# Fillers on a matrix of ones from the start, two of the first four attention jobs in layer 1's buffers, and x's halves squared apart

## The chip, the core and the metric

The kernel runs on one core of one Trainium2 chip. TensorE (PE) multiplies into eight PSUM banks; VectorE (DVE), ScalarE (ACT) and GpSimd (POOL) do the element work; SyncE (SP) issues every DMA. The metric is device time in microseconds for one launch. The time before is the median of three runs.

## What is computed

The reference is attention with decay followed by two pairs of dense layers, all in float32:

```python
# q, k, v: 4 batches x 8 heads x 576 x 64, f: 4 x 8 x 576
cum = np.cumsum(np.log(np.clip(f, 1e-4, 1)), axis=-1)
scores = q @ k.T / 8 + cum[..., :, None] - cum[..., None, :]     # causal
attn = exp(scores - max) / (sum + 1e-9)
x = (attn @ v).transpose(0, 2, 1, 3).reshape(2304, 512)
h = x @ w1_in;  x = (h * sigmoid(h)) @ w1_out        # 512 -> 2048 -> 512
h = x @ w2_in;  x = (h * cos(h)) @ w2_out            # 512 -> 2048 -> 512
```

## The kernel before

**Work and tiles.** Attention is cut into jobs of two heads. Sixteen jobs of kind "a" (four per batch) do the first 256 rows of a sequence as one unit "c01", sixteen of kind "b" the other 320 rows as three units. The tokens are cut into nine tiles of 256; tile j needs the four jobs of its batch and kind. Each of the two layers does, for each tile, eight steps: a step takes 256 columns of the hidden layer, multiplies (line 1282, "h", 24 products), applies the activation, and multiplies into the output (line 1394 in layer 1, line 1183 in layer 2, "y"). Layer 1 runs tiles 0 and 1 step by step beside each other; layer 2 follows layer 1.

**Operands.** Float32 operands that are multiplied as 16-bit ones are split: a high half rounded (name "chi") and a low half, the rest ("clo", for x "xlo", both on line 334). The scale of a split comes from a sum of squares: ScalarE squares with a running sum (line 339), VectorE adds two of those ("sc", line 406), TensorE sums them over partitions by a product with a matrix of ones (line 410, tile "nrm"), VectorE makes powers of two of it (lines 415 to 417). Weights come as 64-bit words and are put into float32 by an exponent shift ("cexp", ScalarE or GpSimd, line 314 or 316), a low-bits step ("cb1", line 462 or 465) and two VectorE steps (lines 468 and 472).

**A unit of attention** (`unit_tasks`): TensorE makes the scores into two PSUM banks "st" (line 746, after mask rows of line 740), VectorE adds the decay, writes the weights tile "e" and keeps the extreme (line 757, "max"), ScalarE takes the exponentials with their sums (line 777), VectorE the reciprocals (lines 783 and 784), then the normalisation goes to GpSimd, VectorE or ScalarE ("nm", lines 314 and 316), TensorE transposes (line 794, "tt"), ScalarE or VectorE copies ("pt"), TensorE multiplies with v (line 928, "pv"), and the product goes to x. For jobs 0 to 3 the decays do not come by DMA: TensorE spreads them ("dp", line 690) as soon as the cumulated sums are there (line 433), and ScalarE copies them ("dk").

**What sets the order.** Each step is a task with an engine (or a choice of engines), a planned duration, a key, the tasks that it waits for, and buffers that it takes (`acq`) and gives back (`rel`); how many buffers there are stands in `TOK`: four PSUM banks "s" for scores, decays, transposes, sums and output units alike, two banks "h" for layer 1, four "e", two "x" for the split x tiles. `Scheduler.run` plays the tasks through once while the program is built, against planned times, and takes for each engine the ready task with the lowest key; the order that results is the program, each engine's queue being fixed from then on. The planner has a rule for TensorE's clock: work takes twice its time until a stretch of it was busy enough. Where TensorE has nothing ready between the planned times `FILL0` and `FILL1`, it gets a filler product `turn` (line 391, tile "spin", bank y0), whose result nobody reads:

```python
    def turn():
        nc.tensor.matmul(spin, identb, one.unsqueeze(1).to_broadcast([128, 2, 256]), start=True, stop=True, ...)
```

**x.** `split_tasks` makes the two halves of an x tile: two squares, one scale, then for each 512-column half a "chi" and an "xlo". Tiles 0 and 1 are written by jobs 0 to 7 straight into SBUF ("x_165", "x_166" in the order), two jobs for each half.

Of the kernel before, what the change touches and what calls it, by code (L numbers as in the profile page):

```python
# [9 lines left out]
F32 = mybir.dt.float32  # L10
# [27 lines left out]
QD = 3  # L38
W1 = 32
CK2 = 20  # L40
FILL0 = 8.0
FILL1 = 60
GAP4, GAP8 = 8, 16
CK0, CK1 = 4, 1.4
# [17 lines left out]
LAND = {"cload": 2.0, "w2l": 1.5, "ldq": 1.5, "ldd": 2.0, "xd": 2.0, "ldx": 1.5, "xt": 1.5}  # L62
ENG = ("PE", "ACT", "DVE", "POOL", "SP")
NEG = -8.0e9
MK2 = -1500.0
EARLY, LATE = 110, ()
KDEC, KDP = 12.0, -0.5
# [10 lines left out]
class Scheduler:  # L78
# [36 lines left out]
    def run(self):  # L115
# [4 lines left out]
        busy = {e: 0.0 for e in ENG}  # L120
        dma_free, lanes, wake = 0.0, [], 0.0
        events, cnt, done = [], 0, 0
        warm, win, work, two = False, 0, [0.0], 0.0

        def push(t, kind, x):
            nonlocal cnt
# [40 lines left out]
        while events:  # L167
# [17 lines left out]
            while progress:  # L185
                progress = False
                for e in ENG:
# [37 lines left out]
                    if e == "PE":  # L225
                        w = int(now / HAM)
                        while win < w:
                            warm = work[win] > 0.7 * HAM
                            win += 1
                            if len(work) <= win:  # L230
                                work.append(0.0)
                        if not warm:
                            end += best.dur
                        a = now
                        while a < end - 1e-9:
                            w = int(a / HAM + 1e-9)
                            while len(work) <= w:
                                work.append(0.0)
                            b = min(end, (w + 1) * HAM)
                            work[w] += b - a  # L240
                            a = b
# [22 lines left out]
def c_dve(n, psum=False):  # L264
    return (0.13 if psum else 0.07) + n / 960
# [31 lines left out]
def decay_attention_silu_cos_kernel(ctx, tc, qa, qb, f, w1i, w1o, w2i, w2o, out):  # L297
# [90 lines left out]
    spin = ps.tile([128, 512], F32, tag="y0", bufs=1, name="spin")  # L388

    def turn():  # L390
        nc.tensor.matmul(spin, identb, one.unsqueeze(1).to_broadcast([128, 2, 256]), start=True, stop=True,  # L391
                         skip_group_check=True)
    sd.keep_warm(0.215, turn)

# [316 lines left out]
    def unit_tasks(jb, kind, pos, split, rel):  # L711
# [7 lines left out]
        dma = jb.kind == "b" and jb.x  # L719
        cell = {}  # L720

        def bank(name):
            return ps.tile([128, 512], F32, tag="s", bufs=TOK["s"], name=name)

        def f_s():
            cell["sm"] = sbt("su", [128, 16])
            for a in range(2):
                st[a] = bank("st")
            for a in range(heads):
                e[a] = sbt("e", [128, S], name="e")  # L730
            if tail:
                for n, (x, y) in enumerate(PASS):
                    mm(st[0][:, 0:256], jb.tail[x], jb.k[y][:, 0:256], start=n == 0, stop=n == 2, skip_group_check=True)  # L733
# [115 lines left out]

        i = pos  # L850
        pe = {"c01": 0.9 if jb.n < ND else 0.72, "c2": 0.5, "c3": 0.67, "T": 0.76}[kind]
        ts = add("PE", pe, f_s, split + [masked], key=i - 10000.0, acq=["s", "s"] + ["e"] * heads + ["su"], rel=rel, name="S")
        te, tm = [], []
        for a in range(2):
            d = {"c01": 0.78, "T": (0.45, 0.52)[a]}.get(kind, c_dve(w) + 0.15)
            hidden = [] if tail and not a else jb.masked[kind]
            t = add("DVE", d, lambda a=a: f_max(a), hidden + ([ts] if not (tail and a) else [ts, t]), key=i + 0.1 * a, rel=["s"],
                    name="max")
            tm.append(t)
            if not tail or a:  # L860
                h = 0 if tail else a
                te.append(add("ACT", (0.9 if kind == "c01" else c_act(w) + 0.19), lambda h=h: f_exp(h), [t], key=i + 0.1 * h,
                              name="exp"))
# [16 lines left out]
        for a in range(0 if dma else heads):  # L880
            tn = []
            for j, (o, n) in enumerate(((0, 128), (128, 256)) if kind == "c01" else ((0, w),)):
                k = 2 * a + j if kind == "c01" else a
                def nf(eng, a=a, o=o, n=n, k=k):
                    return lambda: f_norm(eng, a, o, n, k)
                tn.append(add("POOL", c_pool(n, True), nf("POOL"), [tr], key=i + 0.1 * a, name="nm",
                              alts=[("DVE", c_dve2(n), nf("DVE")), ("ACT", c_act(n) + 0.09, nf("ACT"))]))
            nb = 5 if tail else w // 128
            t = add("PE", 0.115 * nb, lambda a=a: f_t(a), tn + [jb.first], key=i + 0.1 * a - 15000.0,
                    acq=["s"] * (2 if tail else 1) + (["pt"] if kind in ("c01", "c3") and a == 0 else []), rel=["e"],  # L890
                    name="T")
            jb.first = jb.first or t
            for h in range(2 if tail else 1):
                b = h if tail else a
                n = (512, 128)[h] if tail else w
                r.append(add(**copies(lambda b=b: dst(b), lambda b=b: src(b), n, ("ACT", "DVE"), psum=True),
                             deps=[t], key=i + 0.1 * a, rel=["s"], name="tc"))
# [61 lines left out]
    for kind, b in ORDER:  # L959
        if kind == "a":  # L960
            pos += {1: GAP4, 2: GAP8}.get(b, 0)
        for hp in range(H // 2):
# [3 lines left out]
            jb.pt = jb.xo = jb.first = jb.qk = None  # L966
            jb.mate = mate if kind == "a" and hp % 2 else None
            mate = jb
            sp = load_tasks(jb, pos)
            if kind == "a":  # L970
                jb.un = unit_tasks(jb, "c01", pos, sp, [])
                jb.end = pv_tasks(jb, pos + 1, jb.un)
                if jb.mate:
                    add("SP", 0.0, lambda: None, jb.un + jb.mate.un, key=-300, rel=["dk", "qk"])
                    add("SP", 0.0, lambda: None, [jb.end, jb.mate.end], key=-300, rel=["v"])
                pos += 2
            else:
                un = []
                for i, u in enumerate(("c3", "c2", "T")):
# [124 lines left out]
    def split_tasks(l, j, deps, key):  # L1104
# [5 lines left out]
        def make():  # L1110
            x_t[l, j] = sbt("x", [128, 2, KD, TB], F16, "x")
        r = []
        q = [add(**squares(lambda c=c: raw(c), 512, sq[:, c, k:k + 1]), deps=deps, key=key, name="sqx") for c in range(2)]
        ts = scale_tasks(k, q, key)
        tm = add("SP", 0.0, make, [ts], key=-300, acq=["x"])
        for c in range(2):
# [353 lines left out]
```

## Time and profile before

| | us |
|---|---|
| median of 3 runs | 919.29 (917.72 to 922.87) |
| the profiled execution | 919.6 |
| its span | 917.6 |
| TensorE busy in it | 902.0 |
| first TensorE instruction | 6.59 |
| first layer-1 product | 50.89 |

The page gives the busy time of each engine over the span; the stage table gives it for stretches of it. A stretch in which TensorE is busy throughout can still hold fillers, or products at half the clock. The chain of waits follows the work that ended last back from the end; a wait is put down to what released it. Line numbers are those of the kernel before; the change shifts them by 4 to 13.

### The profile page before, as it was taken

Reading aid. Unit: us, or ns where it says so; the run is one execution under the profiler, and the core shown is the slowest. Engines: PE = TensorE matmul, PEld = TensorE weight load, DVE = VectorE, ACT = ScalarE, POOL = GpSimd, SP = SyncE. Lnnn points to the kernel's source line nnn. Section 1 sums busy time; section 2 is a strip of 40 time slices with the busy share of each in tenths; the row PEclk is TensorE's granted clock in tenths of the full one; section 3 lists DMA queues with packets and bytes.
Section 4 is the critical chain, followed back from the end, with each engine's and each line's share of the span. In section 5 each row is a group of like instructions: output and inputs, shape, how many; then the busy total and the mean of one; then the engine's idle time right before and its main releaser. Section 6 shows DMA issues by size and latency. Waiting matters only on the chain.

```text
span 917.6 us, 20983 instructions
## 1 busy us (share of the span) xinstructions
PE 902.0 (98%) x7930; PEld 754.5 (82%) x7930; DVE 768.6 (84%) x1884; ACT 694.2 (76%) x1406; POOL 145.7 (16%) x228
## 2 busy tenths in 40 slices
PE   7998999999999999999999999999999999999997
PEld 4577777777887877878888888888888888888886
DVE  6999989868877999999898966887888888788775
ACT  6999997777877988898787746776676676676663
POOL 5873222112111422232010000000000000000000
PEclk9999999999999999999999999999999999999999
DMA  9876356778996977875756787000001000000010
GB/s 346 296 259 183 90 160 178 172 158 178 205 190 168 255 222 236 201 220 155 241 202 203 261 296 250 27 24 24 25 24 48 25 24 24 1 25 24 1 25 24
DMA packets 113701, 130.03 MB, mean 142 GB/s; under 512 B 63872, under 2 KB 76160, under 8 KB 113600
## 3 DMA queue, kind: packets, MB, share of 16 engines
q1 hardware_dynamic: 113600, 128.70, 48.7%
q8 instruction: 62, 1.02, 0.5%
q14 instruction: 39, 0.32, 0.1%
HBM read 90.25 MB, written 24.72 MB: 125 GB/s over the span
## 4 chain that ended last, share of the span: by engine, by line
PE 90%; DVE 4%; ACT 3%; DMA 2%; issue 1%; POOL 0%; SPq 0%; DVEq 0%; ACTq 0%; POOLq 0%
PE h L1282 38%; PE y L1394 19%; PE y L1183 18%; PE pv L928 3%; PE spin L391 2%; PE tt L794 2%; PE st L753 2%; PE pv L917 2%; PE st L746 2%; PE dp L690 1%; PE st L734 1%; DMA v<-qb 1%; PE st L733 0%; DVE eh L818 0%; ACT junk L339 0%
## 5 line engine op out<-in xcount | busy, mean ns | idle before, releaser
L1282 PE MATMUL h<-x,wi 128*128 128x256 f16 x3456 | 407.5, 273 | 0.0
L1282 PEld LDWEIGHTS <-wi 128*128 128x128 f16 x3456 | 334.2, 98 | 46.5 <-issue 6.7
L1394 PE MATMUL y<-g,rw 128*128 128x256 f16 (+1 forms) x1600 | 224.8, 292 | 0.5 <-ACT g L314 0.5
L1183 PE MATMUL y<-wo,g 128*128 128x256 f16 x1512 | 176.4, 273 | 0.0
L1183 PEld LDWEIGHTS <-g 128*128 128x128 f16 x1512 | 147.9, 98 | 17.1
L1394 PEld LDWEIGHTS <-rw 128*128 128x128 f16 x1344 | 129.3, 98 | 18.2 <-issue 3.1
L1336 ACT ACTIVATE t<-h,ru 128x512 f32<-128x512 f32 x72 | 49.4, 685 | 68.4 <-PE h L1282 68.3
L777 ACT ACTIVATE e<-e,su 128x128 f32<-128x128 f32 (+4 forms) x144 | 82.6, 576 | 9.2 <-DVE su L757 8.0
L1361 DVE TENSOR_TENSOR g<-t,g 128x896 f16<-128x896 f32 x72 | 78.4, 1089 | 10.0 <-ACT g L1358 6.5
L1342 ACT ACTIVATE t<-t,ru 128x512 f32<-128x512 f32 x72 | 51.7, 718 | 37.2 <-DVE t L1339 37.2
L1346 DVE SCALAR_TENSOR_TENSOR t<-h,rg,t 128x512 f32<-128x512 f32 x72 | 53.9, 749 | 29.7 <-ACT t L1343 29.5
L1339 DVE SCALAR_TENSOR_TENSOR t<-t,ru,h 128x512 f32<-128x512 f32 x72 | 53.6, 745 | 24.5 <-ACT t L1336 24.4
L1358 ACT ACTIVATE g<-t 128x896 f16<-128x896 f32 x72 | 67.5, 937 | 6.5 <-DVE t L1352 6.3
L757 DVE CUSTOM_DVE_ANT_0 e<-st,dk 128x256 f32<-128x256 f32 (+3 forms) x144 | 64.3, 477 | 7.5 <-PE st L753 2.8
L1307 ACT ACTIVATE t<-h,rg 128x512 f32<-128x512 f32 x72 | 48.8, 678 | 27.5 <-PE h L1282 26.9
L314 ACT ACTIVATE g<-t,rg 128x512 f16<-128x512 f32 (+1 forms) x70 | 50.1, 716 | 23.9 <-PE y L1394 18.6
L1310 DVE SCALAR_TENSOR_TENSOR t<-t,h 128x512 f32<-128x512 f32 x72 | 49.2, 683 | 15.2 <-ACT t L1307 14.7
L1394 PEld LDWEIGHTS y<-g,rw 128*128 128x128 f32 x256 | 46.7, 194 | 11.0 <-issue 3.4
L334 DVE SCALAR_TENSOR_TENSOR g<-t,rg,g 128x512 f16<-128x512 f32 x56 | 43.2, 772 | 12.9 <-ACT g L314 12.5
L1343 ACT ACTIVATE t<-t,halfpi 128x512 f32<-128x512 f32 x72 | 52.0, 722 | 2.3
L818 DVE SCALAR_TENSOR_TENSOR eh<-e,su,eh 128x512 f16<-128x512 f32 (+2 forms) x66 | 40.5, 639 | 2.9 <-ACT eh L314 2.3
L316 POOL TENSOR_SCALAR e<-e,su 128x128 f32<-128x128 f32 (+3 forms) x38 | 24.7, 656 | 68.0 <-DVE su L784 33.9
(157 smaller groups left out, 1259.7 us busy)
## 6 DMA issues: line engine op xcount, KB each, us to landing
rw<-w1i SPq DMA_DIRECT2D x16, 512.0 KB, 4.5
rw<-w1o SPq DMA_DIRECT2D x16, 512.0 KB, 8.7
x<-x_d SPq DMA_DIRECT2D x16, 512.0 KB, 4.2
dk<-decay_d SPq DMA_DIRECT2D x16, 512.0 KB, 4.8
raw<-w2i SPq DMA_DIRECT2D x16, 512.0 KB, 5.7
raw<-w2o SPq DMA_DIRECT2D x16, 512.0 KB, 4.8
qs<-qb SPq DMA_DIRECT2D x16, 480.0 KB, 4.0
w2o_d<-w SPq DMA_DIRECT2D x24, 256.0 KB, 3.5
```

The lines of the kernel that those rows point to most:

```text
L314: nc.scalar.activation(dst, src, AF.Copy, scale=scale)
L757: nc.vector.tensor_tensor_reduce(out, s, d, -0.125, first, ALU.add, ALU.min, cell["sm"][:, o:o + 1])
L777: nc.scalar.activation(x, x, AF.Exp, bias=sm[:, i:i + 1], scale=-1.0, accum_out=sm[:, 4 + i:5 + i])
L1183: nc.tensor.matmul(y[bank][:, 256 * half:256 * half + 256], g[:, gi, ga], w[:, wi, 256 * col:256 * col + 256], start=p == 0 and half == 0 ...
L1282: nc.tensor.matmul(h[:, i], w[:, wi, 128 * k:128 * k + 128], x[:, xi, k], start=(i == 0 and q == 0 and k == 0), stop=(i == 1 and q == 2 an ...
L1339: nc.vector.scalar_tensor_tensor(cell["t"], cell["t"], r, cell["h"], ALU.subtract, ALU.subtract)
L1342: nc.scalar.activation(cell["t"], cell["t"], AF.Abs, scale=r)
L1343: nc.scalar.activation(cell["t"], cell["t"], AF.Sin, scale=-2.0 * PI, bias=halfpi)
L1346: nc.vector.scalar_tensor_tensor(cell["t"], cell["h"], r, cell["t"], ALU.mult, ALU.mult)
L1358: nc.scalar.activation(g_t[s][:, 0], cell["w"], AF.Copy)
L1361: nc.vector.tensor_tensor(g_t[s][:, 1], cell["w"], g_t[s][:, 0], ALU.subtract)
L1394: nc.tensor.matmul(y[:, e * TB:(e + 1) * TB], w[:, wi, 128 * ec:128 * ec + 128], g[:, gi, i * TB:(i + 1) * TB], start=(st and e == 0), sto ...
```

## The change

- Fillers: `FILL0` goes from 8.0 to 1.5, and the filler multiplies the matrix of ones with itself in place of the identity and the mask tile, so it needs VectorE's first memset alone (GpSimd writes the identity).
- The planner's clock rule: full speed comes after two busy stretches in a row in place of one.
- `ABREAST = (1, 3)`: jobs 1 and 3 take their scores in the two "h" banks and their weights in one of the two "x" buffers, in place of two "s" banks and two "e" tiles; the x buffer is given back once both heads' transposes are done.
- The planned duration of "max" in a c01 unit goes from 0.78 to 0.6.
- `split_tasks`: with four jobs behind a tile, the squares of half c wait for jobs 2c and 2c+1 alone.
- `HEAD = 0` is added and does nothing at that value.

```diff
-FILL0 = 8.0
+FILL0 = 1.5
+HEAD = 0
+ABREAST = (1, 3)
...
-                            warm = work[win] > 0.7 * HAM
+                            full2 = work[win] > 0.7 * HAM
+                            warm = full2 and (warm or half)
+                            half = full2
...
-        nc.tensor.matmul(spin, identb, one.unsqueeze(1).to_broadcast([128, 2, 256]), start=True, stop=True,
+        nc.tensor.matmul(spin, ones16, ones16.unsqueeze(1).to_broadcast([128, 4, 128]), start=True, stop=True,
...
+        early = kind == "c01" and jb.n in ABREAST
...
-                st[a] = bank("st")
+                st[a] = bank("st") if not early else ps.tile([128, 512], F32, tag="h", bufs=2, name="st")
+            both = sbt("x", [128, 2, KD * TB], F16, name="e").bitcast(F32) if early else None
-                e[a] = sbt("e", [128, S], name="e")
+                e[a] = both[:, a] if early else sbt("e", [128, S], name="e")
...
-        ts = add("PE", pe, f_s, split + [masked], key=i - 10000.0, acq=["s", "s"] + ["e"] * heads + ["su"], rel=rel, name="S")
+        ts = add("PE", pe, f_s, split + [masked], key=i - 10000.0, acq=["h", "h", "x", "su"] if early else ["s", "s"] + ["e"] * heads + ["su"],
+                 rel=rel, name="S")
-            d = {"c01": 0.78, "T": (0.45, 0.52)[a]}.get(kind, c_dve(w) + 0.15)
+            d = {"c01": 0.6, "T": (0.45, 0.52)[a]}.get(kind, c_dve(w) + 0.15)
...
+            if early:
+                add("SP", 0.0, lambda: None, [t, jb.first], key=-300, rel=["x"] if a else [])
...
-        q = [add(**squares(lambda c=c: raw(c), 512, sq[:, c, k:k + 1]), deps=deps, key=key, name="sqx") for c in range(2)]
+        q = [add(**squares(lambda c=c: raw(c), 512, sq[:, c, k:k + 1]), deps=deps[2 * c:2 * c + 2] if len(deps) == 4 else deps, key=key,
+                 name="sqx") for c in range(2)]
```

Three places show how the order moves. First the start of TensorE's queue; dp is the spread of the decays, st a score bank. Before:

```order
L690 MATMUL dp_202<-cum_163,sel_158 128x256 x2
L690 MATMUL dp_211<-cum_163,sel_158 128x256 x2
L740 LDWEIGHTS one_133
L740 MATMUL st_226<-one_133 128x2x128
...
L746 MATMUL st_246<-qk_168 128x256
```

After (the first two rows stand there ten times):

```order
L395 LDWEIGHTS ones16_136
L395 MATMUL spin_159<-ones16_136 128x512
L694 MATMUL dp_214<-cum_163,sel_158 128x256 x2
L694 MATMUL dp_223<-cum_163,sel_158 128x256 x2
L747 LDWEIGHTS one_133
L747 MATMUL st_236<-one_133 128x2x128
...
L753 MATMUL st_256<-qk_168 128x256
```

Ten fillers stand ahead of the first decays; up to the first layer-1 product 79 others follow, where 99 stood before.

Second, VectorE's queue behind the scores of jobs 0 and 1 (su_225 and su_244 before, su_235 and su_254 after, hold those jobs' sums; st_333, st_306 are job 2's scores, st_326 and st_327 job 3's; rw are weights in conversion). Before:

```order
L783 TENSOR_SCALAR su_225<-su_225 128x4
L784 RECIPROCAL su_225<-su_225 128x4
L406 SCALAR_TENSOR_TENSOR sq16_140<-sq_139 128x1
L468 SCALAR_TENSOR_TENSOR rw_199<-rw_199 128x512
L415 TENSOR_SCALAR inv_142<-nrm_296 128x1
L416 TENSOR_SCALAR scl_141<-inv_142 128x1
L417 TENSOR_SCALAR inv_142<-inv_142 128x1
L472 SCALAR_TENSOR_TENSOR rw_199<-rw_199 128x512
L468 SCALAR_TENSOR_TENSOR rw_214<-rw_214 128x512
L468 SCALAR_TENSOR_TENSOR rw_222<-rw_222 128x512
L757 ISA e_335,su_332<-st_333,dk_265 128x128
```

After:

```order
L421 TENSOR_SCALAR inv_142<-inv_142 128x1
L476 SCALAR_TENSOR_TENSOR rw_208<-rw_208 128x512
L764 ISA e_308,su_305<-st_306,dk_270 128x128
...
L764 ISA e_309,su_305<-st_307,dk_270 128x256
...
L764 ISA e_328,su_325<-st_326,dk_270 128x128
...
L790 TENSOR_SCALAR su_254<-su_254 128x4
L791 RECIPROCAL su_254<-su_254 128x4
L764 ISA e_328,su_325<-st_327,dk_270 128x128
...
L472 SCALAR_TENSOR_TENSOR rw_221<-rw_221 128x512
```

Two conversions that stood ahead of job 2's scores now stand behind those of jobs 2 and 3. Up to the first "xlo" VectorE has the same rows in both, save one row of line 472 and one set of lines 406 and 415 to 417 less.

Third, TensorE's queue where three sums of squares (nrm) stand among layer 1's output products (y). Before:

```order
L1394 MATMUL y_943<-g_1017,rw_326 128x256 x2
L410 LDWEIGHTS ones16_136
L410 MATMUL nrm_1138<-sq16_140,ones16_136 128x1
...
L410 MATMUL nrm_1152<-sq16_140,ones16_136 128x1
L1394 MATMUL y_942<-g_1148,rw_353 128x256 x2
L1394 MATMUL y_942<-g_1148,rw_365 128x256 x2
...
L410 MATMUL nrm_1182<-sq16_140,ones16_136 128x1
L1394 MATMUL y_943<-g_1148,rw_353 128x256 x2
L1282 LDWEIGHTS wi_1173
L1282 MATMUL h_1192<-x_674,wi_1173 128x256
```

After:

```order
L1407 MATMUL y_866<-g_990,rw_348 128x256 x2
L1407 MATMUL y_867<-g_990,rw_322 128x256 x2
L1407 MATMUL y_867<-g_990,rw_348 128x256 x2
L1407 MATMUL y_866<-g_1110,rw_369 128x256 x2
L414 LDWEIGHTS ones16_136
L414 MATMUL nrm_1122<-sq16_140,ones16_136 128x1
L1407 MATMUL y_866<-g_1110,rw_390 128x256 x2
L1407 MATMUL y_867<-g_1110,rw_369 128x256 x2
...
L414 MATMUL nrm_1145<-sq16_140,ones16_136 128x1
L1407 MATMUL y_867<-g_1110,rw_390 128x256 x2
...
L414 MATMUL nrm_1167<-sq16_140,ones16_136 128x1
```

The first two sums stood back to back; now four output products stand between them, and the first stands behind 26 output products from the start of layer 1 where it stood behind 24. Between the first layer-1 product and this place the other rows are the same in number.

Further counts from the order: up to GpSimd's first mask on a decay tile (line 612), its 256-wide normalisations go from 3 to 8, its 128-wide ones from 8 to 6, its exponent and low-bits steps from 40 to 39. Ahead of ScalarE's twelfth activation of layer 1 (line 1307) there are 2 exponentials of 512 columns, 4 narrow normalisations, 2 squares of v, 4 weight halves and 2 halves of x more, and 6 wide normalisations, 1 transposed copy, 2 halves of v and 1 exponent step less. Ahead of VectorE's twelfth (line 1310) there are 2 score rows of 512 and 2 of 384 columns, 2 low halves of weights, 2 narrow normalisations, 1 transposed copy and 2 halves of v more, 2 high halves of weights and 2 of x less, and some ten rows of a few elements more.

## Rows read from the trace of the kernel before

**Rows 1.** The page's first part: busy us, share of the span, instructions.

```profile
PE 902.0 (98%) x7930; PEld 754.5 (82%) x7930; DVE 768.6 (84%) x1884; ACT 694.2 (76%) x1406; POOL 145.7 (16%) x228
```

**Rows 2.** By stage: length, PE, PEld, DVE, ACT, POOL busy (count), clock, DMA share, GB/s.

```profile
0.00:20.00 20.00, 13.41 (x55) 7.86 (x56) 11.18 (x35) 13.32 (x32) 10.16 (x20) 1.00 0.90 334
...
80.00:100.00 20.00, 17.47 (x109) 13.92 (x109) 19.69 (x65) 18.62 (x49) 3.49 (x6) 0.91 0.22 60
...
120.00:140.00 20.00, 19.94 (x153) 15.19 (x151) 17.71 (x68) 18.58 (x55) 4.26 (x6) 1.00 0.57 176
140.00:160.00 20.00, 20.00 (x142) 15.71 (x142) 18.23 (x55) 15.17 (x35) 4.92 (x9) 1.00 0.63 176
```

**Rows 3.** Groups by line, TensorE: count, busy us, mean ns, idle before.

```profile
L391 PE MATMUL spin<-one 128*128 128x512 bf16 x99 | 23.8, 381 | 0.0
```

**Rows 4.** Chain of waits, first 60 us: start, us, what.

```profile
6.59 3.74 PE dp L690 x8
...
10.87 1.59 PE st L746 x8
...
15.31 1.92 PE dp L690 x8
...
20.82 0.86 PE st L746 x8
...
27.93 2.70 PE spin L391 x12
...
50.89 0.98 PE h L1282 x8
```

**Rows 5.** Timeline of VectorE near 47 us: start, us, what.

```profile
47.50 2.05 DVE L334 SCALAR_TENSOR_TENSOR x<-x,scl,x 128x512 f16<-128x512 f32 x2
```

**Rows 6.** Waits of VectorE, 7.0 to 47.5 us: total us, times, longest.

```profile
DVE inv L415 <- PE nrm L410: 2.2, 3, 1.1
DVE e L757 <- PE st L746: 1.8, 3, 1.0
DVE rw L468 <- ACT rw L462: 1.6, 1, 1.6
```

**Rows 7.** Groups by line and shape, VectorE, 7.0 to 47.5 us.

```profile
L472 DVE SCALAR_TENSOR_TENSOR w<-rw 128x512 int32<-128x512 int32 x6 | 5.3, 884 | 0.1
...
L415 DVE TENSOR_SCALAR inv<-nrm 128x1 int32<-128x1 int32 x4 | 0.6, 154 | 2.2 <-PE nrm L410 2.2
```

**Rows 8.** Groups by line and shape, ScalarE, 6.0 to 46.1 us.

```profile
L314 ACT ACTIVATE rw<-rw 128x512 f32<-128x512 f32 x7 | 4.6, 673 | 1.9 <-DMA rw<-w1i 1.5 <-DMA rw<-w1o 0.5
...
L339 ACT ACTIVATE junk<-w 128x512 bf16<-128x512 f32 x6 | 3.7, 618 | 0.0
```

**Rows 9.** Groups by line and shape, GpSimd, 6 to 85 us.

```profile
L316 POOL TENSOR_SCALAR e<-e,su 128x256 f32<-128x256 f32 x3 | 1.4, 475 | 0.4 <-DVE su L784 0.4
```

**Rows 10.** Timeline of VectorE near 79 us; GpSimd idle, then busy (79.22 to 79.95).

```profile
78.73 0.68 DVE L472 SCALAR_TENSOR_TENSOR rw<-rw 128x512 int32<-128x512 int32 x1
79.33 1.14 DVE L472 SCALAR_TENSOR_TENSOR w<-rw 128x512 int32<-128x512 int32 x1
```

**Rows 11.** Timeline of TensorE, 70 to 87 us: start, us, what, idle before and releaser.

```profile
70.92 1.97 PE L1394 MATMUL y<-g,rw 128*128 128x256 f32 x8
...
81.68 0.16 PE L410 MATMUL nrm<-sq,ones 128*128 128x1 bf16 x1 [0.79 <-DVE su L757]
82.94 0.16 PE L410 MATMUL nrm<-sq,ones 128*128 128x1 bf16 x1 [1.10 <-DVE inv L415]
83.63 3.44 PE L1394 MATMUL y<-g,rw 128*128 128x256 f32 x8 [0.52 <-ACT g L314]
```

**Rows 12.** Timeline of VectorE at the first of those waits.

```profile
81.20 0.41 DVE L757 CUSTOM_DVE_ANT_0 e<-st,dk 128x256 f32<-128x256 f32 x1
```

**Rows 13.** TensorE behind the waits: length, busy (count), granted clock, DMA share, GB/s.

```profile
84.00:85.00 1.00, 1.00 (x3) 0.50 0.00 0
```

**Rows 14.** Waits of ScalarE, 100 to 150 us; four more rows hold 1.9 us together.

```profile
ACT xo L314 <- PE pv L928: 2.6, 2, 1.7
```

More of the change, by code (lines that the diff above doesn't have):

```diff
@@ L122, in run @@
         events, cnt, done = [], 0, 0
-        warm, win, work, two = False, 0, [0.0], 0.0
+        warm, half, win, work, two = False, False, 0, [0.0], 0.0
         def push(t, kind, x):
@@ L851, in unit_tasks @@
         pe = {"c01": 0.9 if jb.n < ND else 0.72, "c2": 0.5, "c3": 0.67, "T": 0.76}[kind]
-        ts = add("PE", pe, f_s, split + [masked], key=i - 10000.0, acq=["s", "s"] + ["e"] * heads + ["su"], rel=rel, name="S")
+        ts = add("PE", pe, f_s, split + [masked], key=i - 10000.0, acq=["h", "h", "x", "su"] if early else ["s", "s"] + ["e"] * heads + ["su"],
+                 rel=rel, name="S")
         te, tm = [], []
         for a in range(2):
-            d = {"c01": 0.78, "T": (0.45, 0.52)[a]}.get(kind, c_dve(w) + 0.15)
+            d = {"c01": 0.6, "T": (0.45, 0.52)[a]}.get(kind, c_dve(w) + 0.15)
             hidden = [] if tail and not a else jb.masked[kind]
-            t = add("DVE", d, lambda a=a: f_max(a), hidden + ([ts] if not (tail and a) else [ts, t]), key=i + 0.1 * a, rel=["s"],
-                    name="max")
+            t = add("DVE", d, lambda a=a: f_max(a), hidden + ([ts] if not (tail and a) else [ts, t]), key=i + 0.1 * a,
+                    rel=["h" if early else "s"], name="max")
             tm.append(t)
@@ L889, in unit_tasks @@
             t = add("PE", 0.115 * nb, lambda a=a: f_t(a), tn + [jb.first], key=i + 0.1 * a - 15000.0,
-                    acq=["s"] * (2 if tail else 1) + (["pt"] if kind in ("c01", "c3") and a == 0 else []), rel=["e"],
+                    acq=["s"] * (2 if tail else 1) + (["pt"] if kind in ("c01", "c3") and a == 0 else []),
+                    rel=[] if early else ["e"],
                     name="T")
             jb.first = jb.first or t
+            if early:
+                add("SP", 0.0, lambda: None, [t, jb.first], key=-300, rel=["x"] if a else [])
             for h in range(2 if tail else 1):
@@ L968, in decay_attention_silu_cos_kernel @@
             mate = jb
+            pos -= HEAD * (kind == "a" and b == 0)
             sp = load_tasks(jb, pos)
@@ L975, in decay_attention_silu_cos_kernel @@
                     add("SP", 0.0, lambda: None, [jb.end, jb.mate.end], key=-300, rel=["v"])
-                pos += 2
+                pos += 2 + HEAD * (b == 0)
             else:
```

## The prediction

> **What bounds the kernel now.** I read the page's first part, the table by stages, the groups by line, the chain of waits, and last the waits of single engines. TensorE is busy 902.0 of 917.6 us [rows 1]; the stage table shows where the missing 15.6 us lie: 6.6 in the first 20 us, 2.5 in 80 to 100 us [rows 2], the rest in small pieces and the tail. So the end is the sum of TensorE's rows plus what it wastes, and a busy TensorE hides waste too. 99 filler products ("spin") stand in its queue [rows 3], all ahead of the first layer-1 product; in the chain, 12 of them take 2.70 us [rows 4], 0.22 us each, so 22 us go on nothing. The second hidden waste is the clock. The granted clock reads full there, but the rows do not: eight score rows take 1.59 us at 10.87 and 0.86 at 20.82, eight decay rows 3.74 us at 6.59 and 1.92 at 15.31 [rows 4]. So TensorE ran at the lower of its levels (1.2 against 2.4 GHz) from its first row at 6.59 until about 15 us.
>
> That does not make TensorE the cause of the head. Fillers stand where the others are late. VectorE and ScalarE are little over half busy in the first 20 us, and at 17.7 to 19.7 of 20 us later, until 140 [rows 2]. The first layer-1 row starts at 50.89 us [rows 4] because VectorE writes the low half of x from 47.50 to 49.55 [rows 5]; 1.3 us lie between. The head gets shorter only if VectorE gets there sooner.
>
> **The change part by part.** *Fewer fillers.* The order has 89 instead of 99, and 10 of the 89 stand ahead of the decay rows, where TensorE sat idle until 6.59. Between the decay rows and the first layer-1 row 79 are left. The other rows there are the same (sixteen decay rows, seven score units, 30 transposes, four output units). 20 fewer by 0.22 us are **4.4 us** of TensorE's queue. The ten at the front cost nothing: their operand comes from VectorE's first memset, they would take 0.44 us each at the low level (twice 0.22), 4.4 in all, and end near 5.5 us, while the decay sums are awaited until 6.59. If they began over a microsecond later than that they would push the decay rows by as much.
>
> *Clock.* If the ten raise it before the decay rows, these take 1.92 instead of 3.74 us and the two score groups behind them 0.86 instead of 1.59 [rows 4]: 1.8 + 1.5 = 3.3 us. If not, 0. No row of before has TensorE working ahead of 6.59, so both ends stay; I take 2.2, nearer the full one, since ten full-size products in a row are denser work than what stands there now.
>
> *VectorE up to the low half of x.* Among its waits between 7.0 and 47.5 us are those for the sums' product (2.2), for scores (1.8) and for ScalarE's conversion (1.6) [rows 6]. The waits for scores shrink when the clock is up and two jobs' scores stand abreast, by about 1.5; the first sums' product stands behind two fillers instead of five, about 1.0. Waits on converted weights stay. Ahead of the low half VectorE has one conversion less (0.88 us) and one set of scale rows less (four by 0.15): 1.5 us [rows 7]. So it comes 1.5 + 2.5 = **4.0 us** sooner; bounds are 1.5 (no wait shrinks) and 5.5 (both kinds of wait go whole). ScalarE has ahead of its x rows at least two conversions less (0.67 each) and two squares less (0.62 each), 2.6 us, besides a pair of exponentials [rows 8]; it is no later than VectorE.
>
> *GpSimd.* Up to the first masked decay tile it takes five more 256-wide normalisations, 0.475 us each [rows 9], and gives up two narrow ones and a conversion, about as much time. A VectorE conversion takes 0.68 us beside an idle GpSimd and 1.14 when GpSimd works [rows 10], so the five could cost VectorE up to five by 0.46, 2.3 us, if the three that went had cost it nothing. I take 0. The Trainium skill (SBUF — State Buffer, Who interferes with whom) says that a VectorE instruction with two SBUF inputs and a GpSimd instruction that reads SBUF exclude each other for a whole instruction, which speaks against moving work to GpSimd here. By that rule the five would cost VectorE five by 0.475, 2.4 us, and the sum would be 2.4 us worse; the row's extra 0.46 agrees with the rule, if nothing that went is set against it.
>
> *Buffers.* Jobs 1 and 3 put scores into layer 1's two banks and weights into the two x buffers. Layer 1 first needs them some 25 us later, when scores are read and transposes past: no wait, cost 0. If that cover were gone, the first layer-1 row would wait for a job's transposes and what is ahead of them, a microsecond or two. Squares of x's halves now wait for their own two jobs; two squares (0.62 us each [rows 8]) thus start earlier on ScalarE and none is added.
>
> *First layer-1 row.* TensorE's queue would bring it forward by 4.4 + 2.2 = 6.6, VectorE allows 4.0 + 1.3 of slack = 5.3. I take **5.0**; what fillers remain saved beyond that turns into waits.
>
> *What is late next.* Between 80.9 and 83.63 us TensorE waits three times, 0.79 + 1.10 + 0.52 us [rows 11]: two sums stand back to back in its queue, and the first wants a score bank that VectorE still reads at 81.20 [rows 12]. The clock then falls, granted 0.50 in 84 to 85 [rows 13], and eight output rows take 3.44 us where eight took 1.97 at 70.92 [rows 11]. The stall costs 2.4 + 1.5 = 3.9. In the new order the sums stand behind two more output products (two rows of 0.215 each, 0.9 us), and four such (1.7 us) lie between the first and the second. With TensorE 5.0 and VectorE 4.0 ahead, and 0.3 us more work on VectorE in between, the first sum waits 0.79 - 0.9 + 1.0 + 0.3 = 1.2 us and the others not. If 1.2 us of idleness leaves the clock up, 2.7 are won; if it falls, 1.2. I take **2.0**.
>
> *Up to the twelfth layer-1 step* (147 us) the new order puts more other work ahead: on ScalarE net six full-size rows, 0.67 us each [rows 8], 4.0 us; on VectorE net seven, between 0.41 (a score row [rows 12]) and 0.88 each [rows 7], 2.9 to 6.2, say 4.6. TensorE being 7 ahead, they must find 7 and 4 to 4.6 us by then. Some 4 come from the head; ScalarE has 4.5 us of waits between 100 and 150, 2.6 of them for output products [rows 14], and the steps have room between product and use. I price what is left at **1.0** lost, bounds 0 and 4.6.
>
> *Sum.* -5.0 - 2.0 + 1.0 = **-6.0 us**. The profiled execution took 919.6 us (917.6 of span and 2.0 around it); the median of the three runs is 919.29, so the scales agree within 0.3. 919.6 - 6.0 = **913.6 us**.
>
> **The rivals.** (1) *The fillers become waits.* The clock stays low until 15 us as now (the change then does not do what it says) or VectorE's waits do not shrink. For: TensorE works 8.5 us from its first row before its rows get faster, so a few rows more may not do it; VectorE is full from 20 us on. Then the first layer-1 row gains some 2.5, the stall at 82 us stays: 917.1 us.
> (2) *TensorE's queue decides.* VectorE's waits go whole, the head gains 4.4 + 3.3, of the stall 1.2 is left of 3.9, 1.0 is lost later: -7.7 - 2.7 + 1.0 = -9.4, 910.2 us.
> (3) *Slower: the longer queues at the twelfth step.* If the head gives VectorE only 1.5 us, the 4.6 more ahead of that step make it 3.1 later than now; TensorE waits there for the activation, and the idle clock falls as at 83 us, 1.5 more: 919.6 + 4.6 = 924.2 us. It decides when VectorE's head gain is under 3 and its later waits are not free to give. Against it: ScalarE has waits to give [rows 14] and is down to 15.17 of 20 us in 140 to 160 [rows 2].
>
> **How the numbers follow.** A measurement of this kernel can tell about 0.5%, 4.6 us, from no change. Forecast 0.50 (911 to 915.5 by itself); rival 1 0.25; rival 2 0.13; rival 3 0.12. Faster by over 4.6 us (below 914.7): four fifths of the forecast, 0.40, and rival 2, **0.53**. Slower by over 4.6: the worse part of rival 3, **0.09**. Within: **0.38**. The range goes from rival 2's price, a microsecond more for the unknown clock term, to past rival 1 by GpSimd's 2.3: **909 to 920**.
>
> **What would show it.** Right: ten fillers before 6.6 us and the first eight decay rows near 1.9 us; first scores read by 12 us; the low half of x at 43 to 44 us and the first layer-1 row at 45.5 to 46.5; no row at the low level after 20 us; TensorE idle under 3 us between 20 and 160. Wrong: those decay rows again at 3.7 us (rival 1); waits of TensorE between 20 and 45 us that add up to the fillers saved; a granted clock below full between 75 and 150 us; a layer-1 step near 140 us waiting for ScalarE or VectorE (rival 3).

## The result and the profile after

| | us |
|---|---|
| before, median of 21 runs | 920.75 (917.72 to 925.42) |
| after, median of 21 runs | 925.73 (923.40 to 930.93) |
| ratio after to before | 1.0055, 95% interval 1.0039 to 1.0071 |
| profiled execution after, span | 924.8 (before 917.6) |

The change makes the kernel slower by 0.55%, 5.1 us. The forecast was 913.6, 6 us faster. The times of the kernel before lie in two groups, 917.72 to 920.75 (eleven) and 922.87 to 925.42 (ten), which nothing here explains, so its median moves by a microsecond or two with the share of either.

The page's first part (busy us, share of the span, instructions), to be read beside [rows 1]:

```profile
PE 907.3 (98%) x7920; PEld 753.9 (82%) x7920; DVE 767.4 (83%) x1880; ACT 694.4 (75%) x1409; POOL 151.6 (16%) x229
```

TensorE has ten rows fewer, all of them fillers, and is busy 5.3 us longer: some of its rows ran at the lower clock. Its idle time is 924.8 - 907.3 = 17.5 us, 1.9 more than before. The table by stages says where (length, PE, PEld, DVE, ACT, POOL busy with counts, granted clock, DMA share, GB/s), beside [rows 2]:

```profile
0.00:20.00 20.00, 17.45 (x58) 8.81 (x60) 11.13 (x34) 13.55 (x34) 10.65 (x21) 0.70 0.89 329
...
40.00:60.00 20.00, 18.53 (x139) 11.39 (x139) 17.92 (x56) 17.81 (x53) 17.71 (x23) 1.00 0.73 241
...
80.00:100.00 20.00, 14.70 (x74) 10.30 (x72) 18.94 (x61) 19.37 (x52) 7.12 (x9) 0.83 0.31 103
```

TensorE idles 5.30 us in 80 to 100 us, where it idled 2.53, and 1.47 in 40 to 60, where it idled nowhere; only 74 rows start in 80 to 100, where 109 did. From 100 to 900 us it idles 1.77 (0.83 before).

**The head.** TensorE's timeline (start, us, what, idle before and releaser), beside [rows 4]:

```profile
1.05 4.05 PE L395 MATMUL spin<-ones 128*128 128x512 bf16 x10 [1.05 <-DVE ones L357]
6.60 2.40 PE L694 MATMUL dp<-cum,sel 32*128 32x256 f32 x8 [1.49 <-DVE cum L437]
...
13.19 3.77 PE L694 MATMUL dp<-cum,sel 32*128 32x256 f32 x8
...
51.54 0.61 PE L1295 MATMUL h<-x,wi 128*128 128x256 f16 x4
```

The ten fillers end at 5.10 us and TensorE waits 1.49 us for the sums. The first decay rows begin at the full clock; at about 8.0 us it falls (granted 0.50 until 21.6), and the second eight take 3.77 us, where they took 1.92. The low level lasts longer than before, and the first layer-1 product starts at 51.54 instead of 50.89 with 20 fillers fewer ahead of it.

**The stall at 81 to 84 us**, beside [rows 11], now lies at 86 to 96:

```profile
82.83 0.17 PE L414 MATMUL nrm<-sq,ones 128*128 128x1 bf16 x1
...
84.67 0.17 PE L414 MATMUL nrm<-sq,ones 128*128 128x1 bf16 x1
...
87.42 0.16 PE L414 MATMUL nrm<-sq,ones 128*128 128x1 bf16 x1 [1.61 <-DVE sq L410]
89.01 4.90 PE L1295 MATMUL h<-x,wi 128*128 128x256 f16 x28 [1.43 <-ACT wi L318]
95.83 0.33 PE L801 MATMUL tt<-ident,e 128*128 128x128 f32 x1 [1.93 <-ACT e L318]
```

```profile
90.00:92.00 2.00, 2.00 (x11) 0.50 0.32 127
...
98.00:100.00 2.00, 2.00 (x10) 0.50 0.00 0
```

The two sums that waited before (0.79 and 1.10 us) do not wait any more. The third does, 1.61 us, and behind it the causes are new: a half of a layer-1 weight ("wi") and a normalisation on ScalarE. In all the waits are longer. The clock falls twice behind them; the rows of the second fence are TensorE's by stretches (length, busy, clock, DMA share, GB/s).

### The profile page after: what moved, and what is told of

Its sections match the earlier page's. It is cut to its first block, busy times and chain, and to the rows that moved or that the text cites. A ratio compares the mean times of both kernels' runs of the same rounds, so it can differ in the third digit from the quotient of the medians.

```text
span 924.8 us, 20960 instructions
## 1 busy us (share of the span) xinstructions
PE 907.3 (98%) x7920; PEld 753.9 (82%) x7920; DVE 767.4 (83%) x1880; ACT 694.4 (75%) x1409; POOL 151.6 (16%) x229
## 4 chain that ended last, share of the span: by engine, by line
PE 84%; DVE 6%; ACT 5%; issue 2%; DMA 2%; POOL 2%; SPq 0%; DVEq 0%; POOLq 0%; ACTq 0%
PE h L1295 37%; PE y L1196 18%; PE y L1407 17%; PE pv L939 2%; PE st L760 2%; PE pv L928 2%; PE tt L801 2%; PE st L753 1%; ACT junk L343 1%; ACT e L784 1%; DMA qs<-qb 1%; PE st L741 1%; PE dp L694 1%; PE spin L395 1%; DVE rw L472 1%
## 5 line engine op out<-in xcount | busy, mean ns | idle before, releaser
L1407 PE MATMUL y<-g,rw 128*128 128x256 f16 (+1 forms) x1600 | 221.5, 291 | 0.2 <-ACT g L318 0.2
L1349 ACT ACTIVATE t<-h,ru 128x512 f32<-128x512 f32 x72 | 49.3, 685 | 68.7 <-PE h L1295 68.6
L1352 DVE SCALAR_TENSOR_TENSOR t<-t,ru,h 128x512 f32<-128x512 f32 x72 | 53.6, 744 | 24.5 <-ACT t L1349 24.4
L1407 PEld LDWEIGHTS y<-g,rw 128*128 128x128 f32 x256 | 45.7, 190 | 8.5 <-issue 2.5
L825 DVE SCALAR_TENSOR_TENSOR eh<-e,su,eh 128x512 f16<-128x512 f32 (+1 forms) x66 | 41.6, 656 | 3.8 <-ACT eh L318 2.8
L343 ACT ACTIVATE junk<-w 128x512 bf16<-128x512 f32 x48 | 29.9, 624 | 5.3 <-DVE w L476 4.3
```

The source lines that it names most:

```text
L1352: nc.vector.scalar_tensor_tensor(cell["t"], cell["t"], r, cell["h"], ALU.subtract, ALU.subtract)
L1407: nc.tensor.matmul(y[:, e * TB:(e + 1) * TB], w[:, wi, 128 * ec:128 * ec + 128], g[:, gi, i * TB:(i + 1) * TB], start=(st and e == 0), sto ...
```

## The experiments

All ratios are to the kernel before on the same chip, with a 95% interval.

**1. Is it the clock?** The first theory was that the ten fillers raise the clock, the gap of 1.5 us lets it fall, and the low level to 21.6 us costs the time. Four kernels keep an order, instruction for instruction, and change only the fillers at the front: none or sixteen in the changed kernel, ten or sixteen in the kernel before.

```diff
     def turn():
+        calls[0] += 1
+        if calls[0] <= 10:          # none; the version with sixteen issues six more at call 10
+            return
         nc.tensor.matmul(spin, ones16, ...)
```

> The changed kernel's order, instruction for instruction, without the ten fillers ahead of the decay rows (79 fillers left, all behind them). Theory H (the clock in the head): in the changed kernel the fillers raise the clock, TensorE then stands idle for 1.5 us, the clock falls at about 8 us and stays at the low level until 21.6, where the kernel before has it up at about 15; so without them the clock comes up near 15 us again, the decay rows take 3.7 us, the first layer-1 row comes at 48 to 50 us instead of 51.5, and the time is 919 to 922 us. Rival O (the new order): two jobs abreast, more normalisations on GpSimd and the other queues of VectorE and ScalarE cost the time, and the ten fillers are neutral: 924 to 928 us.

> The changed kernel's order with sixteen fillers ahead of the decay rows instead of ten, so that TensorE works without a gap from 1.1 us up to the decay rows (16 by 0.42 or, once the clock is up, 0.22 us each: they end between 6.5 and 7.5). Theory H: with the gap of 1.5 us closed the clock stays up through the decay rows and the scores (decay rows 1.9 us, score rows 0.86), the first layer-1 row comes at 47 to 49 us, and the time is 915 to 920 us. If the clock falls at 8 us all the same, it is not the gap but the thin work behind it, and the time is that of the changed kernel, 925. Rival O: clock up or not, 924 to 927 us.

> The kernel before, its order unchanged, with ten fillers on ones put ahead of its first decay rows. Theory H: the clock rises at about 5 to 6 us, falls at 8 and stays low until some 20 us: 923 to 926 us. Rival O: the fillers are neutral or gain a little: 918 to 921 us.

> The kernel before, its order unchanged, with sixteen fillers on ones ahead of its first decay rows, no gap up to them. Theory H: if the clock holds, decay rows 1.9 us and the following scores 0.86, no low level before 20 us, 916 to 920 us; if it falls at 8 us all the same, 923 to 926. Rival O: within 1.5 us of the kernel before, 920.7.

| kernel | ratio |
|---|---|
| changed, none | 1.0058 (1.0037 to 1.0079) |
| changed, ten (the change) | 1.0055 (1.0039 to 1.0071) |
| changed, sixteen | 1.0049 (1.0030 to 1.0069) |
| before, ten | 1.0005 (0.9985 to 1.0025) |
| before, sixteen | 0.9995 (0.9977 to 1.0012) |

The theory falls: the loss stays whatever the clock does in the head, and the fillers alone cost the kernel before nothing that shows. Without fillers the low level lasted until some 23 us and not, as I expected, until 15, and the first layer-1 product came at 53.1 us; with sixteen it came at 48.3; yet the two ratios differ by 0.1%. The kernel before with sixteen has the full clock up to 20 us and gains nothing that shows. Its stages:

```profile
0.00:20.00 20.00, 18.37 (x91) 9.35 (x91) 13.26 (x36) 15.26 (x38) 11.03 (x21) 1.00 0.89 333
20.00:40.00 20.00, 18.56 (x120) 9.89 (x120) 17.72 (x50) 17.52 (x52) 18.69 (x21) 1.00 0.97 344
...
80.00:100.00 20.00, 16.44 (x111) 12.72 (x110) 19.69 (x65) 18.29 (x49) 4.51 (x6) 1.00 0.21 59
```

TensorE's time saved becomes 1.44 us of waiting in 20 to 40 and 1.0 more in 80 to 100.

**2. Which part of the order?** Each of four parts was taken back alone in the changed kernel; the planner then orders everything anew.

```diff
-ABREAST = (1, 3)                                       # a_noabreast
+ABREAST = ()
-            d = {"c01": 0.6,                           # a_max78
+            d = {"c01": 0.78,
-                            warm = full2 and (warm or half)   # a_clockrule
+                            warm = full2
-  deps=deps[2 * c:2 * c + 2] if len(deps) == 4 else deps      # a_halves
+  deps=deps
```

> The changed kernel with no job's scores and weights in layer 1's banks and x's buffers (the list ABREAST empty), the rest of the change kept; the planner then orders the whole anew. Theory A (the abreast jobs cost it: more weights to be normalised at once, GpSimd takes ten wide ones up to 97 us instead of five and TensorE waits for them at 47 to 50 us and for weights and squares at 81 to 97): without them TensorE's waits at 81 to 97 us come down from 5.3 to about the 2.5 of the kernel before, 919 to 922 us. Rival P (the planner's costs, its clock rule and 0.6 for a maximum of scores, put the queues of VectorE and ScalarE in a worse order): stays at 924 to 927 us. Either way ten fillers at the front.

> The changed kernel with the planner's cost of a job's maximum of scores at 0.78 again. Theory A: 924 to 927 us, the stall at 81 to 97 us as large as in the changed kernel. Rival P: 919 to 922 us.

> The changed kernel with the planner's old rule for TensorE's clock (full as soon as one stretch was busy). Theory A: 924 to 927 us. Rival P: 919 to 922 us.

> The changed kernel with the squares of x's two halves waiting for all four jobs again instead of their own two. Theory A: 924 to 927 us. Rival P, and a third view (the earlier squares stand on ScalarE ahead of normalisations that are awaited): 919 to 922 us only if those squares are what is late.

| taken back | ratio |
|---|---|
| jobs abreast | 1.0046 (1.0024 to 1.0067) |
| cost 0.6 | 1.0072 (1.0051 to 1.0093) |
| clock rule | 1.0058 (1.0035 to 1.0081) |
| squares apart (a_halves) | 0.9988 (0.9967 to 1.0008) |

Neither theory A (the abreast jobs) nor P (the planner's costs) is borne out: no part that they name gives the time back. Taking back the smallest part of the diff, which I had priced at nothing, does. Each of the four is a new order throughout, so this step does not yet tell the part from the order that comes with it.

**3. That part alone, and each x tile for itself.** b_halves is the kernel before with this one line. a_first and a_second keep it for one x tile only (`len(deps) == 4 and j == 0`, or `j == 1`). a_halves_bridge has it taken back and sixteen fillers, the order otherwise that of a_halves.

> The kernel before with one part of the change alone: the square of each half of x waits only for its own two jobs. Theory Q (the early square stands on ScalarE ahead of a job's exponentials and of weights that are awaited, and what it is for, the sum over both halves, cannot start before the second half): slower, 923 to 926 us, with waits of TensorE for weights or squares between 45 and 100 us. Rival R (the planner's order is a draw: any small edit sends the later queues elsewhere, by some microseconds either way): anything between 916 and 926, and no early square in the chain of cause; near 920 if the draw is neutral.

> The changed kernel with the halves apart only for the first x tile (squares at 30 and 42 us), together again for the second. Theory Q: the square at 30 us is the one that delays a job's exponentials, 923 to 927 us. Rival R: no relation, anything between 917 and 928.

> The changed kernel with the halves apart only for the second x tile (a square at about 59 us), together for the first. Theory Q with the first square as the culprit: 918 to 921 us. If the second square, ahead of layer-1 weights at 60 to 75 us, is it: 923 to 927. Rival R: anything between 917 and 928.

> The changed kernel with the squares of the halves waiting for all four jobs, its order unchanged, and sixteen front fillers instead of ten, so that no gap stands ahead of the decay rows. If the low clock from 8 to 21 us costs anything once the squares are out of the way: 916 to 918 us, faster than both kernels. If VectorE and ScalarE set the head whatever the clock is: 918.5 to 920.5, the same as with the ten.

| kernel | ratio |
|---|---|
| before with the squares apart | 1.0088 (1.0060 to 1.0116) |
| changed, first tile alone apart | 1.0081 (1.0049 to 1.0113) |
| changed, second tile alone apart | 1.0021 (1.0001 to 1.0041) |
| changed, together, sixteen fillers | 0.9955 (0.9938 to 0.9973) |

The part alone makes the kernel before slower by 0.9%. In the changed kernel the first tile alone costs 0.9% against a_halves, the second alone 0.3%, and both together 0.7%: the parts do not add up, as each version is planned anew, and theory Q and rival R cannot be told apart here. The last kernel beats both: 917.62 us beside 921.96 before. (The kernel before took longer on this chip than the 919.9 to 920.8 of the others; between the medians of a_halves, 919.65 on its chip, and of this one lie 2.0 us.) Its head, its layer-1 products up to 100 us (count, duration, first to last start) and its stage:

```profile
1.05 5.35 PE L404 MATMUL spin<-ones 128*128 128x512 bf16 x16 [1.05 <-DVE ones L357]
6.59 1.96 PE L703 MATMUL dp<-cum,sel 32*128 32x256 f32 x8 [0.18 <-DVE cum L446]
...
11.06 1.99 PE L703 MATMUL dp<-cum,sel 32*128 32x256 f32 x8
```

```profile
L1304 PE MATMUL h<-x,wi x167: 269/273/283, 45.6 to 100.0; 128*128 128x256 f16 x167
```

```profile
60.00:80.00 20.00, 18.81 (x118) 14.37 (x115) 19.76 (x43) 19.18 (x48) 15.07 (x16) 1.00 0.85 272
80.00:100.00 20.00, 17.16 (x128) 13.82 (x127) 19.79 (x63) 18.52 (x53) 9.56 (x9) 1.00 0.27 86
```

The first layer-1 product starts at 45.6 us; the kernel before has 144 such products started by 100 us, the changed one 128, this one 167. Of the 5.2 us by which it starts earlier than before, 3.0 are left in the span (914.6 against 917.6). One score unit less stands ahead of it, six instead of seven, and that work comes later; and TensorE now waits 1.19 us in 60 to 80, and 2.84 in 80 to 100.

**4. The square itself, or what the planner puts behind it?** ScalarE's timeline after is, up to 30.3 us, that of a_halves; then it has the early square where a_halves has the fourth job's second exponentials:

```profile
29.85 0.50 ACT L784 ACTIVATE e<-e,su 128x256 f32<-128x256 f32 x1
...
30.34 0.62 ACT L343 ACTIVATE junk<-x 128x512 bf16<-128x512 f32 x1
...
31.06 1.20 ACT L318 ACTIVATE e<-e,su 128x128 f32<-128x128 f32 x3
32.17 0.39 ACT L784 ACTIVATE e<-e,su 128x128 f32<-128x128 f32 x1
```

The exponentials come at 32.17 instead of 30.38 us. a_late moves only the early squares, beside their sisters, in the changed order; ah_early moves only the first square, ahead of those exponentials, in a_halves' order; every other row keeps its place on every engine. a_late_bridge is a_late with sixteen fillers, and ah_noabreast_bridge is a_halves_bridge planned anew with no job abreast.

```diff
+                def both():                # a_late: the first square waits in "held" for the second
+                    held.append(fn)
+                    if len(held) == 2:
+                        for f in held:
+                            f()
...
+            if kind == "c01" and jb.n == 3 and a == 1:     # ah_early, ahead of f_exp's rows
+                x_t["ahead"]()
```

> The changed kernel's order, instruction for instruction, except that the early square of each x tile stands on ScalarE beside its sister (11 and 16 us later), where it stood before the change. Theory Q1 (the 0.8 us of the square itself, ahead of a job's second exponentials, is the cost): 919 to 922 us. Theory Q2 (the square's freedom changes what the planner puts after it, on all engines, and that order is the cost): 924 to 927 us, as the changed kernel.

> The order of the changed kernel with the squares together, except that the first square of the first x tile stands ahead of the fourth job's second exponentials, where the changed kernel has it. Q1: 923 to 926 us. Q2: 919 to 921 us, as with the squares together.

> The changed kernel's order with the early squares beside their sisters and sixteen front fillers. Q1: 916 to 919 us, as the kernel with the squares together and sixteen fillers (917.6 there beside 922.0 of the kernel before). Q2: 922 to 925 us.

> Squares together, sixteen front fillers, and no job abreast: scores of all jobs in the score banks again. If the abreast jobs are what lets VectorE start sooner once the clock is up: first layer-1 row at 48 to 50 us instead of 45.6, and 918 to 921 us. If they are neutral: 915 to 918 us and the first row near 46.

| kernel | ratio |
|---|---|
| changed order, squares late | 1.0053 (1.0032 to 1.0073) |
| a_halves' order, first square early | 0.9984 (0.9964 to 1.0003) |
| changed order, squares late, sixteen | 1.0037 (1.0018 to 1.0055) |
| together, sixteen, no job abreast | 1.0095 (1.0069 to 1.0121) |

Q2 holds, in both directions: the place of the square is worth nothing beyond the intervals (0.2%), and the order that the planner makes once it may be early is the loss. The last row shows that the squares are not alone in this: another replanned order, with the squares together, is as slow as any. It took 929.75 us, outside both of my ranges, with the first layer-1 product at 49.3.

**What the slow orders share.** TensorE's waits in 20 to 160 us were read for eighteen profiles. In the twelve of a ratio over 1.002 TensorE waits for a weight half (wi) or for a normalisation on ScalarE; in the six of a ratio under 1.001 (the kernel before among them) it waits for neither. In 80 to 100 us it idles 4.57 to 8.34 us in the twelve and 2.32 to 3.56 in the six; in 300 to 500 us 0.12 to 4.03 in the twelve and at most 0.61 in the six. First b_halves, then a_halves_bridge (waiter, releaser, total us, times, longest; 20 to 160 and 20 to 100 us):

```profile
PE h L1283 <- ACT wi L314: 3.0, 1, 3.0
PE tt L794 <- ACT e L314: 1.8, 1, 1.8
PE nrm L410 <- DVE su L757: 1.8, 2, 1.4
PE y L1395 <- ACT g L314: 1.7, 1, 1.7
```

```profile
PE nrm L423 <- DVE su L773: 1.6, 1, 1.6
PE tt L810 <- POOL e L320: 1.4, 2, 0.9
PE y L1416 <- ACT g L318: 1.2, 1, 1.2
PE nrm L423 <- DVE sq L419: 1.1, 2, 0.6
```

So a slow order goes with a TensorE that runs out of work between 80 and 100 us, where the rows name ScalarE and VectorE as late with weights, sums and normalisations; b_halves has 11.66 us of TensorE work in that stage and a clock of 0.75. No run makes those weights alone earlier, so that they are the cause is not shown. In the changed kernel one step lies at 46 us: three normalisations on GpSimd take 3.38 us, 1.1 each (1.84 for three at 46.10 before), and TensorE's transposes wait for them.

```profile
46.23 3.38 POOL L320 TENSOR_SCALAR e<-e,su 128x128 f32<-128x128 f32 x3
```

```profile
47.48 0.55 PE L801 MATMUL tt<-ident,e 128*128 128x128 f32 x3 [0.40 <-POOL e L320]
...
49.66 0.44 PE L801 MATMUL tt<-ident,e 128*128 128x128 f32 x2 [1.07 <-POOL e L320]
```

ScalarE's copies wait in turn, 5.8 us for transposes between 20 and 97 us, and 3.5 in a_halves.

**5. The clock in the head, a second time.**

> The changed kernel once more, for one profile: is the clock in the head (down at 8 us, up at 21.6) a property of the kernel, or drawn anew in each execution? If of the kernel: decay rows in 2.4 us, low level from 8 to about 21.6 again. If drawn: another pattern, with the first layer-1 row between 46 and 52 us accordingly, while TensorE's idle time in 80 to 100 us stays at 4.5 to 6 us.

> Squares together and sixteen front fillers once more, for one profile: if closing the gap holds the clock dependably, decay rows in 1.96 us and full level up to 22 us again, first layer-1 row at 45.6; if it was luck, a drop between 8 and 20 us and a first row at 47 to 50.

The changed kernel took 929.22 us, the other 916.27, the kernel before 918.50 on that chip. The head of the changed kernel in its second profile:

```profile
1.05 4.45 PE L395 MATMUL spin<-ones 128*128 128x512 bf16 x10 [1.05 <-DVE ones L357]
6.59 3.75 PE L694 MATMUL dp<-cum,sel 32*128 32x256 f32 x8 [1.09 <-DVE cum L437]
...
14.53 3.77 PE L694 MATMUL dp<-cum,sel 32*128 32x256 f32 x8
```

The decay rows behind the fillers ran at the low level here, and the first layer-1 product came at 53.08 us. So the head differs from one execution of the same program to the next. With sixteen fillers the decay rows took 1.99 us again, and the first product came at 46.35. Stages 80 to 100 are as before: 5.51 us idle here, 2.93 there.

## Why the prediction was wrong

- **What is late next (-2.0): the step that failed.** I counted output products ahead of the sums in the two orders and let the wait shrink. That much came, and more: the first two sums do not wait at all, where I had left 1.2 us. But I did not ask whether what TensorE takes behind them would be there, and the third sum, the next weight half and the next job's transposes wait 1.61, 1.43 and 1.93 us. TensorE idles 5.30 us in 80 to 100 instead of 2.53, and the clock is low for some 7 us in place of some 3, half of which is lost: 2.8 + 2, so 4.8 us lost where I had 2.0 won. In the fastest kernel the idle time there is 2.84, no less than before, but its clock stays up: eight output rows behind the waits take 1.99 us (87.75) instead of 3.44.
- **x's halves (priced at 0).** This is the part of the diff that goes with that loss, a term put at nothing without a look at what follows it. I wrote that two squares start earlier "and none is added", as if an edit of what a task waits for moved that task alone. Its order is made by a planner, and 0.67% lies between the changed kernel and the one with this line taken back, 6 us. The squares themselves are free, as I said; the order behind them is not.
- **Clock term (2.2 of 0 to 3.3).** In the changed kernel's two profiles the first decay rows take 2.40 and 3.75 us, not 1.9. With sixteen fillers they take 1.96, and the scores 0.93 (the same length in this view as the 0.86 of the chain); with ten, three of the other orders had 1.96 too. That the ten end by 5.5 us and TensorE then stands idle was in my own sum; I priced two thirds of the full clock all the same. What it is worth is small: 0.1% in the kernel before, 0.1 to 0.2% in the changed order, 0.3% with the squares together (0.9988 to 0.9955, on two chips), and the intervals of each pair overlap.
- **Fewer fillers (-4.4), VectorE (-4.0), first layer-1 row (-5.0).** In the changed kernel the row starts at 51.54 instead of 50.89. VectorE begins the low half of x at 47.19, 0.3 us earlier instead of 4.0: its waits for scores grew from 1.8 to 2.4 us, 2.25 of them at 21.38 behind slow rows, where I had taken 1.5 off. And VectorE did not decide: it is done with that half by 48.8, and TensorE, which waits 0.40 and 1.07 us for GpSimd's normalisations, gets to the row 2.8 us later. In the kernel before, too, TensorE had no wait for that half: it was busy for the whole of 20 to 60 us. With sixteen fillers the changed order has the row at 48.3 (47.8 with the squares late), so some 2.5 to 3 of the 5.0. The 45.6 and 46.3 of the kernel with the squares together lie in the forecast's range, but in another order, with a score unit less ahead of the row; they do not confirm the sum.
- **GpSimd (0, bound 2.3).** Up to 97 us VectorE's first conversion step (line 472, 468 before) takes 0.90 us in the mean instead of 0.87, but the second (476, 472 before) 0.78 instead of 0.86, so VectorE lost nothing. GpSimd did: its 256-wide normalisations take 0.75 us instead of 0.47, its 128-wide ones 0.71 instead of 0.65, and TensorE waits 1.47 us for those at 46 us. I had not priced that engine. But a_halves, no slower than the kernel before, has 0.72 and 0.70, so this price alone is not the loss.
- **Buffers (0).** The first layer-1 product follows the row ahead of it without a wait; right as far as this row shows. That two jobs' scores stand abreast was one of my two reasons for 1.5 us less of VectorE's waits; without it the best kernel is 1.4% slower and the changed kernel the same, which shows two replanned orders rather than the worth of the buffers.
- **Up to the twelfth step (+1.0; rival 3).** Rival 3 had the sign, and ScalarE and VectorE late with the clock falling behind. Its number, 924.2, came close by luck: its place was 140 us and its wait was for the activation, but in 100 to 160 us TensorE idles 0.09 us; the loss fell at 87 to 96, for weights, a sum and normalisations. I had given it 0.12, and my range ended short of it.

In the profiled execution the sum is: 5.3 us more busy (0.6 in fillers, 23.8 to 24.4 us for ten fewer, as more of them ran slow; some 2 in 80 to 100; the rest in the slow head) and 1.9 more idle, 7.2. By place, 6.9 of the 7.2 are lost by the first output product of layer 2, 575.3 us instead of 568.4. The measured 5.1 goes by 21 executions of each kernel, 923.40 to 930.93 and 917.72 to 925.42 us; the profiled ones are one of each.

What stays open: why a planner that may place a square earlier ends with weights later. All seven orders planned with the squares apart came out slower (one by 0.2%, barely clear of 1), but so did one with them together; whether that freedom is bad in itself, or each new order is a draw between 0.9955 and 1.0095, these runs cannot tell.

## What to carry to other kernels

Where a program orders the queues, every edit of a dependency, a cost or a buffer is a new order: cost it by comparing what each engine has done by the next stall, above all the operands that the bound engine takes after it, and separate the edit from the order by moving the instruction alone. Fillers that end ahead of the first real product left the clock up for it in some executions and not in others; bridging the gap held it for the decay rows in all six profiles here, and won 0.3% at most. Time saved ahead of a stall counts only as far as the engines behind that stall are earlier too.

## What the runs showed of the hardware

- With the same ten fillers from 1.05 us and a gap of 1.1 to 1.8 us, the profiles show the head in many ways: full until 8.0 us and low until 21.6, low from 9.6 to 12.4 (ah_early), or the low level from the first decay row until 23. The first eight decay rows took 1.96 us in three of eleven such profiles. ah_early and a_halves, of one order but for one square, took 917.34 and 921.37 us in their profiled executions, with the first layer-1 product at 45.7 and 49.4. The Trainium skill (TensorE: Matmul & The Clock Gate, Part 1) says that the number of slow products at the start varies from run to run; these rows agree (eight decay rows of the changed kernel took 2.40 and 3.75 us).
- With sixteen fillers and gaps up to 0.47 us all six profiles have the first sixteen decay rows at 1.96 to 1.99 us for eight. In two of them, both with the changed kernel's order, the granted clock then reads 0.50 from 15 to 17 us.
- The granted clock reads 1.00 in a stretch where rows run at the low level all along: in the second profile of the changed kernel eight decay rows take 3.75 us at 6.59, and the column shows no drop. Here it shows when the clock falls, not that it has not risen yet: the rows' own durations have to be read.
